# A routed feed-forward behind attention: two listed tiles of two halves for three whole ones, and the last tile's output scattered in two pieces

## The chip, the cores and the metric

The kernel runs on one core of one Trainium2 chip. The metric is the device time of one execution in microseconds; lower is better. The time to compare with is the median of three runs. The engines are named as in the profile: PE (TensorE matmuls), PEld (its weight loads), DVE (VectorE), ACT (ScalarE), POOL (GpSimd) and SP (SyncE, which here only issues DMAs).

## The reference

```python
def _attn_ref(q, k, v, g_q, g_k):            # q, k, v: (8, 12, 448, 64)
    q_n, k_n = (rmsnorm(q, g_q), rmsnorm(k, g_k))
    scores = 1.0 / np.sqrt(64) * np.matmul(q_n, k_n.transpose(0, 1, 3, 2))
    ...
    return np.matmul(softmax, v)

def _moe_ref(x, w_gate, w1_dense, w2_dense, w1, w2):   # x: 3584 tokens x 768
    y_dense = np.maximum(x @ w1_dense, 0.0) @ w2_dense  # hidden size 512
    logits = x @ w_gate                                 # 8 experts
    expert_idx = np.argmax(logits, axis=1)
    ...
    for e in range(E):
        mask = expert_idx == e
        h = np.maximum(x[mask] @ w1[e], 0.0)
        y_moe[mask] = gate_w[mask, None] * (h @ w2[e])
    return (y_dense + y_moe).astype(np.float32)
```

Attention of 96 heads gives 3584 tokens of 768 features. Every token goes through a dense feed-forward and through one of eight experts, which its logits choose; the sum of both is written to the output. The inputs are one fixed draw.

## The kernel before, in words

**Two stages.** In the first stage (up to about 230 us) the kernel computes attention, the logits, the choice of the expert and the hidden layer of the dense feed-forward, and writes each token as a record (its 768 features, its 512 dense hidden values, its gate weight and its token number) into a DRAM tensor `records`, sorted by expert: each expert has a region of its own there. In the second stage it reads the records back in tiles of 128, runs the expert on each tile, and scatters the rows of the tile to the output by token number.

**The tiles of the second stage.** Tiles 0 to 15 are the first two full tiles of each expert, 16 to 23 the third one of each. Tiles 24 to 27 are made of two halves: 64 records of one expert and 64 of its neighbour. What an expert has beyond 3 1/2 tiles (448 tokens) goes to *listed* tiles, which are found at run time: `final_list` (L550) counts the tokens of each expert and `listed` (L491) writes, for each listed tile, the number of the expert (`expt`) and the place of its records (`unit`). Before the change a listed tile is 128 records of one expert, `ND` = 3 of them are always run (tiles 28, 29 and 30), and more would be run in `surplus` under a branch at the end (L997), which is taken if more than `ND` are listed.

**What one tile does.** `fetch` (L774) reads the place of the tile on SP and issues its DMAs: for most tiles one load of the records, which `turn` (L795) transposes on PE; for the late tiles a small load (gate weight and token number, L782) and a transposing DMA (L783). `gemm1` (L816) makes the hidden layer: for tiles 3 to 27 with the expert's weights standing (L838), for listed tiles with the tokens standing and the weights moving (L829, six matmuls of 512 columns); their expert's number is read into a register on PE, and the weights are addressed through it. `htrans` (L843) transposes the hidden layer of a listed tile (PE L852, ACT L853). `gemm2` (L855) runs eight matmuls of 384 columns for the dense part (L862) and as many for the expert (L873; sixteen of 64 tokens each, in pairs, where a tile has two halves). DVE then writes the sum to `ysb` (L881 for listed tiles, L883 for the others), and POOL scatters it to `out` (L886).

**The order.** Every engine runs its instructions in the order in which the program issues them. In `tiles` (L900) the step for tile t issues the fetch of tile t+4 or t+5, `turn` of t+2, `gemm1` of t+1, `gemm2` of t and `htrans` of t+1. The steps before tile 3 are in the hand-written order `AT["tail"]`, where `li` issues the instructions of `final_list`, on DVE, in three portions. `pair()` hands out two pairs of PSUM banks in turn, so that who writes a pair waits until the one before the last that used it has been read.

## Time and profile before

| | us |
|---|---|
| median of 3 runs | 371.98 |
| lowest and highest run | 369.56, 372.89 |
| the profiled execution | 369.48 |
| its span, from the first to the last instruction | 367.7 |
| mean granted TensorE clock, share of full speed | 0.997 |

The profile belongs to one execution. Its span is 1.8 us shorter than its time. Times of single instructions below count from the start of the span.

### The profile page before, as it was taken

The page shows a single profiled execution, that of the slowest core. Times are in us where ns is not written, and L with a number is a line of the kernel's source. Part 1 is how long each engine was busy: PE and PEld are TensorE (multiplying, and loading weights), DVE is VectorE, ACT ScalarE, POOL GpSimd, SP SyncE. Part 2 cuts the span into 40 slices and gives each one's busy share as a digit, 9 for nine tenths or more (in the row PEclk, how much of TensorE's full clock was granted, in tenths as well). Part 3 has the DMA queues.
Part 4 walks back from the last instruction along what each step waited for, and adds up shares of the span by engine and source line. Part 5 has one row for each costly group of instructions (what it writes and reads, how often), then busy time and mean ns, then how long its engine had stood idle before and what let it go on. Part 6 is the DMA issues. An engine that isn't in the chain of part 4 may idle for free. (4 is left out here: it accounts for less than half of the span.)

```text
span 367.7 us, 11921 instructions
## 1 busy us (share of the span) xinstructions
PE 328.4 (89%) x4715; PEld 220.9 (60%) x4715; DVE 219.4 (60%) x793; ACT 230.6 (63%) x365; POOL 214.0 (58%) x300
## 2 busy tenths in 40 slices
PE   0367889999899998999999988999999999999992
PEld 0145566665575655656656654677777777777651
DVE  4778999888798888978866354523332432222221
ACT  2368988998889988989888333444443543334330
POOL 7357687868987689879689053437613512232222
PEclk9999999999999999999999999999999999999998
DMA  5969999999999879993269999888994966557410
GB/s 193 304 204 191 296 279 237 309 296 290 274 296 277 287 207 205 328 274 131 68 113 214 263 277 226 299 294 267 307 288 107 259 182 191 151 149 194 132 71 31
DMA packets 55438, 82.38 MB, mean 224 GB/s; under 512 B 18412, under 2 KB 43500, under 8 KB 55376
## 3 DMA queue, kind: packets, MB, share of 16 engines
q1 hardware_dynamic: 43184, 44.29, 42.2%
q0 software_dynamic: 12192, 37.27, 38.5%
q8 instruction: 39, 0.64, 0.7%
q14 instruction: 23, 0.19, 0.2%
HBM read 69.31 MB, written 26.97 MB: 262 GB/s over the span
## 5 line engine op out<-in xcount | busy, mean ns | idle before, releaser
L332 ACT ACTIVATE xflat<-PS 128x896 bf16<-128x896 f32 x168 | 146.0, 918 | 20.8 <-PE PS L330 18.9
L284 POOL TENSOR_TENSOR xn<-weall,r 128x448 bf16<-128x448 f32 x91 | 83.1, 939 | 9.0 <-issue 3.2
L886 POOL DMA_INDIRECT out_dram<-xflat,rall x31 | 30.6, 989 | 88.9 <-DVE xflat L883 46.0
L330 PE MATMUL PS<-qT,kT 64*128 64x448 bf16 x384 | 70.0, 366 | 10.7 <-ACT xflat L332 8.3
L349 PE MATMUL PS<-va,xflat 128*128 128x65 bf16 (+1 forms) x1536 | 75.9, 195 | 1.2 <-DVE rall L375 0.5
L349 PEld LDWEIGHTS <-xflat 128*128 128x128 bf16 (+1 forms) x1536 | 60.4, 97 | 23.1 <-issue 13.5
L263 DVE BATCH_NORM_STATS2 st<-weall 128x6 f32<-128x128 f32 x336 | 70.9, 279 | 4.0 <-DMA weall<-in_k_dram 3.7
L883 DVE SCALAR_TENSOR_TENSOR xflat<-PS,rall,xflat 128x768 f32<-128x768 f32 x25 | 25.4, 1018 | 77.2 <-ACT xflat L866 38.0
L479 POOL DMA_INDIRECT records<-rall,slot x32 | 32.6, 1018 | 23.9 <-ACT rall L612 13.1
L862 PE MATMUL PS<-wd,xflat 128*128 128x384 bf16 x248 | 45.5, 326 | 0.8 <-ACT heT L853 0.8
L873 PE MATMUL PS<-weall,heT 128*128 128x384 bf16 (+2 forms) x280 | 45.5, 327 | 0.2 <-ACT heT L853 0.2
L607 PE MATMUL PS<-wd,xT 128*128 128x512 bf16 x168 | 41.1, 380 | 1.2 <-ACT rall L612 1.2
L330 PEld LDWEIGHTS <-kT 64*128 64x128 bf16 x384 | 22.4, 95 | 27.7 <-issue 22.3
L838 PE MATMUL PS<-xflat,weall 128*128 128x128 bf16 (+1 forms) x696 | 38.7, 213 | 0.0
L375 DVE TENSOR_TENSOR rall<-PS,inv 128x256 bf16<-128x256 f32 x96 | 36.2, 419 | 2.0 <-DVE inv L381 0.4
L838 PEld LDWEIGHTS <-weall 128*128 128x128 bf16 x696 | 36.4, 115 | 1.5 <-issue 0.9
L873 PEld LDWEIGHTS <-heT 128*128 128x128 bf16 (+1 forms) x280 | 24.3, 100 | 16.7 <-issue 1.3
L842 ACT ACTIVATE heT<-PS 128x512 bf16<-128x512 f32 x25 | 14.9, 597 | 30.5 <-PE PS L838 28.9
L866 ACT COPY xflat<-PS 128x768 f32<-128x768 f32 x25 | 20.0, 799 | 18.9 <-PE PS L862 14.1
L295 PE MATMUL PS<-ident,xn 64*128 64x64 bf16 x672 | 17.8, 194 | 15.3 <-DVE xn L284 12.2
L862 PEld LDWEIGHTS <-xflat 128*128 128x128 bf16 x248 | 23.0, 98 | 13.9 <-issue 1.0
L803 ACT COPY xflat<-PS 128x512 bf16<-128x512 bf16 x22 | 12.9, 585 | 24.1 <-PE PS L802 24.0
(129 smaller groups left out, 347.2 us busy)
## 6 DMA issues: line engine op xcount, KB each, us to landing
weall<-in_q_dram SPq DMA_DIRECT2D x24, 448.0 KB, 8.9
weall<-in_k_dram SPq DMA_DIRECT2D x11, 896.0 KB, 10.2
rall<-records SPq DMA_DIRECT2D x18, 352.0 KB, 7.7
weall<-in_v_dram SPq DMA_DIRECT2D x48, 128.0 KB, 3.5
weall<-in_moe_w_dram POOLq DMA_DIRECT2D x8, 768.0 KB, 10.9
weall<-in_v_dram SPq DMA_DIRECT2D x48, 96.0 KB, 5.4
weall<-in_moe_w_dram POOLq DMA_DIRECT2D x12, 256.0 KB, 10.3
weall<-in_moe_w_dram POOLq DMA_DIRECT2D x8, 384.0 KB, 9.8
```

Of the source, the lines that this page charges most:

```text
L263: return [lambda s=s: nc.vector.bn_stats(sts[g][:, "qk".index(name), s].rearrange("p h c -> p (h c)"), xin[name, g].rearrange("p h (s d) - ...
L284: (eng or nc.gpsimd).tensor_tensor(xn[name, g][:, :, hh], xin[name, g][:, hh].rearrange("p (s d) -> p s d", d=D), r[:, "qk".index(name), : ...
L330: nc.tensor.matmul(ps[:, hh, :S], kT[row, c:c + P], qT[row, r], start=(n == 0), stop=(n == len(mm) - 1), skip_group_check=True)
L332: nc.scalar.activation(x, ps[:, :, :S], AF.Exp, scale=scale)
L349: nc.tensor.matmul(av[:, hh, m], exs[g, s][rows_, hh, QC[m]:QC[m] + P], va[rows_, s, hh, :De], start=(first and s == full[0] and m == m0), ...
L375: nc.vector.tensor_tensor(x[:, 2 * hh + r], av[:, hh, :, :D].rearrange("p m (a i) -> p m a i", a=2), inv[:, hh].unsqueeze(3).to_broadcast( ...
L479: i = nc.gpsimd.indirect_dma_start(out=rec, out_offset=bass.IndirectOffsetOnAxis(ap=slot[b % 2][:, m:m + 1], axis=0), in_=rb[b % 3][:, m], ...
L607: nc.tensor.matmul(W[:, bank], turnedx(b, kk, m), wd1[:, kk], start=(kk == 0), stop=(kk == KD - 1))
L838: nc.tensor.matmul(he[:, i * P + own.start:i * P + own.stop], weight(t, a, 0, kk * F + i, FT), xRs[t][:, kk, own], start=(i == 0 and a == ...
L862: nc.tensor.matmul(yps[t][:, dd, :HD], xRs[t][:, KD + i], wd2[:, i, dd * HD:(dd + 1) * HD], start=(i == 0), stop=(i == FT - 1 and not one_ ...
L873: nc.tensor.matmul(yp[own, dd, :HD], heTs[t][:, i, own], weight(t, a, 1, i * Dm + dd * HD), start=(i == 0 and not one_sum), stop=(i == FT ...
L886: i = nc.gpsimd.indirect_dma_start(out=out, out_offset=bass.IndirectOffsetOnAxis(ap=got(t)[:, GO + 1:GO + 2].bitcast(I32), axis=0), in_=ys ...
```

## The change

Listed tiles are now made of two halves of 64 records, each with an expert of its own, and two of them are run always (tiles 28 and 29). The list is written in halves, up to 50 of them instead of 27 tiles. The first half of a listed tile uses its expert's weights through a register on PE as before; the weights of the second half's expert are first copied by DVE to a fixed place (`hold`): those of the first layer into `wd1`, those of the second into a part of `xT` (tile 28) or of `rall` (tile 29). In `gemm1` and `gemm2` of listed tiles each matmul of 128 tokens becomes two of 64. The last tile has a `gemm2` of its own, `last_gemm2`: it does the 384 output features of one half after those of the other, and copies and scatters each alone; POOL makes the two row numbers for that.

```diff
--- before.py
+++ after.py
@@ -120,9 +120,9 @@
     EL = 4
     NE, NS = 2 * E, 3 * E
     NM = NS + E // 2
-    ND = 3
+    ND = 2
     LAST = NM + ND
-    NF = N // P - 1
+    NF = 25
     NT = NM + NF
     BLANK = 2 * E * RT
     MAGIC = 12582912.0
@@ -509,7 +508,6 @@
             lambda: ge.tensor_reduce(o[1], t[1], AX.X, ALU.add),
             lambda: ge.tensor_tensor(o[2], o[1], iot[:, :n], ALU.add),
             lambda: ge.tensor_scalar(o[2], o[2], first[:, :1], None, op0=ALU.add),
-            lambda: ge.tensor_scalar(o[2], o[2], 2.0, 1.0, op0=ALU.mult, op1=ALU.add),
             lambda: ge.tensor_scalar(unit[:, row, :n], o[2], float(BLANK), None, op0=ALU.min)]
 
     def counted(b, c):
@@ -564,12 +562,12 @@
             lambda: ve.tensor_scalar(back, took, 2.0, -float(BLANK), op0=ALU.mult, op1=ALU.add)
         ] + halves(unit[:, 1, :E]) + [
             lambda: ve.tensor_tensor(first, took, one_, ALU.add),
-            lambda: ve.tensor_scalar(last, n, -0.5, 1.0 / P, op0=ALU.add, op1=ALU.mult),
-            lambda: ve.tensor_scalar(last, last, MAGIC, MAGIC, op0=ALU.add, op1=ALU.subtract),
-            lambda: ve.tensor_tensor(last, last, first, ALU.max),
             lambda: ve.tensor_tensor(one_, first, up, ALU.is_lt),
             lambda: ve.tensor_scalar(back, first, 2.0, -float(BLANK), op0=ALU.mult, op1=ALU.add)
-        ] + halves(unit[:, 1, E:2 * E]) + listed(NF, RT, first, last, 2, pre) + [
+        ] + halves(unit[:, 1, E:2 * E]) + rounded(last, n, D, True) + [
+            lambda: ve.tensor_scalar(first, first, 2.0, 1.0, op0=ALU.mult, op1=ALU.add),
+            lambda: ve.tensor_tensor(last, last, first, ALU.max)
+        ] + listed(2 * NF, 2 * RT, first, last, 2, pre) + [
             lambda: ve.tensor_copy(total, pre[:, E - 1:])]
 
     def gaps(ix):
@@ -739,14 +737,15 @@
     SETTLE = (TT + 6, TT + 12, TT + 16, TT + 20, TT + 24, LAST - 2)
     hsur = const.tile([P, FT, P], BF16)
     gix = const.tile([P, E], I32)
+    idx2 = const.tile([P, 2], I32)
 
 
     def parts(t):
-        return [slice(0, D), slice(D, P)] if NS <= order[t] < NM else [slice(0, P)]
+        return [slice(0, D), slice(D, P)] if order[t] >= NS else [slice(0, P)]
 
     def place(t, a):
         return ((0, t) if t < NE else (1, t - NE) if t < NS else (1, E + 2 * (t - NS) + a)
-                if t < NM else (2, t - NM))
+                if t < NM else (2, 2 * (t - NM) + a))
 
     def expert(t, a=0):
 
@@ -769,7 +768,7 @@
 
     def by_dma(t):
 
-        return t >= NS - 3 and len(parts(t)) == 1
+        return t >= NS - 3 and not NS <= order[t] < NM
 
     def fetch(t):
         xRs[t] = xrb[t % 5]
@@ -780,7 +779,7 @@
             r = r.rearrange("o p c -> (o p) c")
             if by_dma(t):
                 ins = [nc.sync.dma_start(got(t)[own, GO:GO + 2], r[:, GO:GO + 2]),
-                       nc.sync.dma_start_transpose(xRs[t], r[:, :GO].bitcast(BF16))]
+                       nc.sync.dma_start_transpose(xRs[t][:, :, own], r[:, :GO].bitcast(BF16))]
             else:
                 ins = [nc.sync.dma_start(got(t)[own], r)]
             e = expert(order[t], a)
@@ -802,12 +801,30 @@
                 nc.tensor.transpose(o[:, k], x[:, a * KD + k], ident)
             copy(xRs[t][:, a * KD:a * KD + n], o)
 
+    def other(t):
+
+
+        w2 = (xT.rearrange("p k n s -> p (k n s)")[:, :FT * Dm].rearrange("p (i d) -> p i d", i=FT)
+              if t % 2 == 0 else rall[:, 7:11, :GO].bitcast(BF16)[:, :, :Dm])
+        return wd1, w2
+
+    def hold(t):
+
+        n = 2 * (t - NM) + 1
+        e = nc.vector.value_load(expt[:, 2, n:n + 1], min_val=0, max_val=E - 1)
+        for n, w in enumerate(other(t)):
+            nc.vector.tensor_copy(w, we[:, bass.ds(e, 1), n].rearrange(
+                "p o (i f) -> p (o i) f", i=w.shape[1]))
+
     def weight(t, a, n, c, step=1):
 
         w = step * (P - 1) + 1 if step > 1 else F if n == 0 else HD
         e = expert(order[t], a)
         if e is not None:
             return we[:, e, n, c:c + w:step]
+        if a:
+            i, c = divmod(c, F if n == 0 else Dm)
+            return other(t)[n][:, i, c:c + w]
         return we[:, bass.ds(eregs[t], 1), n, c:c + w].rearrange("p o f -> p (o f)")
 
     def token_major(t):
@@ -815,8 +832,8 @@
 
     def gemm1(t, heT=None):
         if t >= NM:
-            eregs[t] = nc.tensor.value_load(expt[:, 2, t - NM:t - NM + 1], min_val=0,
-                                            max_val=E - 1)
+            n = 2 * (t - NM)
+            eregs[t] = nc.tensor.value_load(expt[:, 2, n:n + 1], min_val=0, max_val=E - 1)
         heTs[t] = sb.tile([P, FT, P], BF16, tag="qT", name="heT") if heT is None else heT
         if t < TT:
             mids[t] = pair()
@@ -826,8 +843,9 @@
             claim("01"[t % 2], ("he", t))
         if token_major(t):
             for kk in range(KD):
-                nc.tensor.matmul(he, xRs[t][:, kk], weight(t, 0, 0, kk * F),
-                                 start=(kk == 0), stop=(kk == KD - 1))
+                for a, own in enumerate(parts(t)):
+                    nc.tensor.matmul(he[own], xRs[t][:, kk, own], weight(t, a, 0, kk * F),
+                                     start=(kk == 0), stop=(kk == KD - 1))
             hes[t] = sb.tile([P, F], BF16, tag="xv", name="hs")
             nc.scalar.activation(hes[t], he, AF.Relu, scale=gate(t))
         else:
@@ -852,7 +870,32 @@
             nc.tensor.transpose(hp[:, i], hs[:, i], ident)
         nc.scalar.copy(heTs[t], hp)
 
+    def last_gemm2(t):
+
+        ys, yp = ysb[t % 3], pair()
+        for dd in range(2):
+            nc.gpsimd.tensor_scalar(idx2[:, dd:dd + 1], got(t)[:, GO + 1:GO + 2].bitcast(I32),
+                                    2.0, float(dd), op0=ALU.mult, op1=ALU.add)
+        for dd in range(2):
+            for i in range(FT):
+                nc.tensor.matmul(yp[:, dd, :HD], xRs[t][:, KD + i],
+                                 wd2[:, i, dd * HD:(dd + 1) * HD], start=(i == 0), stop=False)
+            for i in range(FT):
+                for a, own in enumerate(parts(t)):
+                    nc.tensor.matmul(yp[own, dd, :HD], heTs[t][:, i, own],
+                                     weight(t, a, 1, i * Dm + dd * HD), start=False,
+                                     stop=(i == FT - 1), skip_group_check=False)
+            nc.vector.tensor_copy(ys[:, dd], yp[:, dd, :HD])
+            i = nc.gpsimd.indirect_dma_start(
+                out=out.rearrange("n (a d) -> (n a) d", a=2),
+                out_offset=bass.IndirectOffsetOnAxis(ap=idx2[:, dd:dd + 1], axis=0),
+                in_=ys[:, dd], in_offset=None, bounds_check=2 * N - 1, oob_is_err=False)
+            apart(i, stores, "each token has one slot")
+            stores.append(i)
+
     def gemm2(t, part=None):
+        if t == LAST - 1:
+            return last_gemm2(t)
 
         one_sum = token_major(t)
         if part != 1:
@@ -911,6 +954,8 @@
                 turn(t + 2)
             if t + 1 < LAST:
                 gemm1(t + 1)
+            if NM <= t + 2 < LAST:
+                hold(t + 2)
             gemm2(t)
             if t + 1 < LAST:
                 htrans(t + 1)
@@ -920,6 +965,7 @@
         for t in range(LAST, NT):
             fetch(t)
             turn(t)
+            hold(t)
             gemm1(t, hsur)
             htrans(t)
             gemm2(t)
@@ -993,8 +1039,8 @@
         attention()
         tail_and_slots()
 
-    ntot = nc.values_load(total, min_val=0, max_val=NF)
-    with tc.If(ntot > ND):
+    ntot = nc.values_load(total, min_val=0, max_val=2 * NF)
+    with tc.If(ntot > 2 * ND):
         with tc.manual_schedule(engines=ENGINES):
             surplus()
```

In the order of the engines, three places show it. First PE, at the start of the first layer of tile 28. Before, six matmuls move the weights of one expert past 128 tokens (`xflat` holds the tokens, `weall` the experts' weights; ISA computes an address from the register):

```order
L818 TENSOR_LOAD expt
L818 ISA x2
L829 LDWEIGHTS xflat
L829 ISA
L829 MATMUL PS<-weall,xflat 128x512
```

Now each has become two of 64 tokens, the second with the weights that DVE has copied into `wd1` (here `wd_81`):

```order
L836 TENSOR_LOAD expt
L836 ISA x2
L847 LDWEIGHTS xflat
L847 ISA
L847 MATMUL PS<-weall,xflat 64x512
L847 LDWEIGHTS xflat
L847 MATMUL PS<-wd_81,xflat 64x512
```

The number of columns that move is the same for each matmul; the number of matmuls has doubled. Second DVE, at the end of its program. Before, the sums of tiles 25, 26 and 27 (L883) stand one behind the other, and then the copies of the three listed tiles:

```order
L803 COPY xflat<-PS 128x768
L883 SCALAR_TENSOR_TENSOR xflat<-PS,rall,xflat 128x768 x3
L881 COPY xflat<-PS 128x768 x3
L996 TENSOR_LOAD total
L997 COMPARE_AND_BRANCH
```

Now a register load and two copies of 3072 elements each stand between the sums of tiles 25 and 26 (`hold` of tile 28):

```order
L926 SCALAR_TENSOR_TENSOR xflat<-PS,rall,xflat 128x768
L814 TENSOR_LOAD expt
L814 ISA x2
L816 ISA
L816 COPY wd_81<-weall 128x3072
L816 ISA
L816 COPY xT<-weall 128x3072
L926 SCALAR_TENSOR_TENSOR xflat<-PS,rall,xflat 128x768
```

The same rows stand again between the sums of tiles 26 and 27 (`hold` of tile 29, with `rall` in place of `xT`), and behind them are one copy of 768 columns (L924, tile 28) and two of 384 (L888, tile 29) where three of 768 were. Third POOL, at the end of its program, before:

```order
L886 DMA out_dram<-xflat,rall 3584x768
L896 DMA weall<-in_moe_w_dram 128x1536
L886 DMA out_dram<-xflat,rall 3584x768 x17
L996 TENSOR_LOAD total
L997 COMPARE_AND_BRANCH
```

and now:

```order
L939 DMA weall<-in_moe_w_dram 128x1536
L929 DMA out_dram<-xflat,rall 3584x768 x15
L877 TENSOR_SCALAR idx_104<-rall 128x1 x2
L889 DMA out_dram<-xflat,idx_104 7168x384 x2
L1042 TENSOR_LOAD total
L1043 COMPARE_AND_BRANCH
```

Two whole scatters are gone, and two small operations and two scatters of half rows stand at the end.

## Rows read from the trace of the kernel before

**Rows 1.** Windows, tiles 3 to 27: length, busy us of PE, PEld, DVE, ACT, POOL; clock

```profile
237.00:345.00 108.00, 108.00 (x1281) 82.09 (x1279) 33.09 (x44) 44.01 (x67) 37.50 (x42) 1.00 0.76 216
```

**Rows 2.** Timeline of the last tiles: start, duration, what, [idle before <-releaser]

```profile
340.90 1.02 DVE L883 SCALAR_TENSOR_TENSOR xflat<-PS,rall,xflat 128x768 f32<-128x768 f32 x1 [3.02 <-ACT xflat L866]
...
344.84 1.46 PE L829 MATMUL PS<-weall,xflat 128*128 x6
345.10 1.02 DVE L883 SCALAR_TENSOR_TENSOR xflat<-PS,rall,xflat 128x768 f32<-128x768 f32 x1 [3.18 <-PE PS L873]
...
346.39 0.98 POOL L886 DMA_INDIRECT out_dram<-xflat,rall  x1 [3.22 <-DVE xflat L883]
...
349.49 1.46 PE L829 MATMUL PS<-weall,xflat 128*128 x6
...
353.61 1.46 PE L829 MATMUL PS<-weall,xflat 128*128 x6
...
357.73 1.46 PE L862 MATMUL PS<-wd,xflat 128*128 128x384 bf16 x8
357.98 0.58 ACT L853 COPY heT<-PS 128x512 bf16<-128x512 bf16 x1 [2.14 <-PE PS L852]
...
359.03 1.46 PE L873 MATMUL PS<-weall,heT 128*128 x8
360.53 0.96 DVE L881 COPY xflat<-PS 128x768 f32<-128x768 f32 x1 [1.86 <-PE PS L873]
361.76 0.98 POOL L886 DMA_INDIRECT out_dram<-xflat,rall  x1 [1.85 <-DVEq L997]
```

**Rows 3.** DMA issues: count, KB, median us from issue to landing

```profile
out_dram<-xflat,rall POOLq DMA_INDIRECT x31, 3.8
...
xflat<-records SPq DMA_TRANSPOSE x9, 3.5
```

**Rows 4.** Timeline around one tile of two halves: PE, and PEld

```profile
308.91 1.46 PE L862 MATMUL PS<-wd,xflat 128*128 128x384 bf16 x8
310.31 1.49 PE L873 MATMUL PS<-weall,heT 128*64 128x384 bf16 x16
311.73 1.79 PE L838 MATMUL PS<-xflat,weall 128*128 128x64 bf16 x48
...
310.30 1.12 PEld L873 LDWEIGHTS <-heT 128*64 128x64 bf16 x16 [0.32 <-issue]
```

**Rows 5.** Lines by form: out<-in count | busy us, mean ns | idle before

```profile
L803 DVE COPY xflat<-PS 128x768 bf16<-128x768 bf16 x22 | 12.1, 549 | 9.3 <-PE PS L802 9.3
L881 DVE COPY xflat<-PS 128x768 f32<-128x768 f32 x6 | 5.7, 958 | 11.4 <-PE PS L873 11.3
L316 DVE COPY kT<-PS 128x128 bf16<-128x128 bf16 x24 | 5.1, 213 | 0.0
...
L504 DVE TENSOR_TENSOR t<-iot,f 1x216 f32<-1x216 f32 x1 | 0.4, 361 | 0.0
```

**Rows 6.** Timeline of PE, DVE and POOL where DVE makes the list

```profile
235.40 0.98 POOL L479 DMA_INDIRECT records<-rall,slot  x1 [1.85 <-ACT rall L612]
...
235.98 0.40 DVE L512 TENSOR_SCALAR o<-o 1x27 f32<-1x27 f32 x1
...
237.69 1.50 PE L838 MATMUL PS<-xflat,weall 128*128 128x128 bf16 x24
237.89 0.96 DVE L881 COPY xflat<-PS 128x768 f32<-128x768 f32 x1
...
239.03 0.72 PE L802 MATMUL PS<-ident,rall 128*128 128x128 bf16 x10
```

**Rows 7.** Timeline of SP's queue: the transposing loads of tiles 28 and 29

```profile
331.10 1.39 SPq L783 DMA_TRANSPOSE xflat<-records  x1
...
335.04 1.37 SPq L783 DMA_TRANSPOSE xflat<-records  x1
```

**Rows 8.** POOL's small operations: times of L447 on one line of the timeline

```profile
221.91 0.22 POOL L447 TENSOR_SCALAR rall<-dbase 128x4 int32<-128x4 f32 x1
```

## Prediction

> **What bounds the kernel now.** I read the windows first: from 237 to 345 us PE is busy in all 108 us, at full clock, while the other engines have room [rows 1]. So in the second stage each microsecond that PE is given or spared comes out at the end. Then I read the timeline of the last tiles [rows 2]. What the reader is to see: PE runs on without a wait from the first listed tile (344.84) to its last block (359.03, which with its 1.46 us ends at 360.49); then come one after the other the DVE copy of the last result (360.53 to 361.49), the issue of its scatter on POOL (361.76 to 362.74), and the landing. The end is thus PE's end plus a chain of about 5 us to the last landing, which is in part the scatter's 3.8 us [rows 3]. The chain of waits says nothing of use here, since it holds only the last scatter.
>
> **Whether the work fits.** By the reference's own choice of experts, counted from its fixed draw in float32, the experts get 409, 528, 432, 430, 448, 366, 478 and 493 tokens. Beyond 448 that is three tiles of 128 (one each for 528, 478, 493), and in halves of 64 it is 2 + 1 + 1 = 4, just what two tiles hold. The trace agrees for the tiles: 31 scatters [rows 3] are 28 tiles and three listed ones, so the branch to `surplus` was not taken, and the expert with 448 did not get a 449th token on the chip. A fifth half would need 19 more tokens for the expert with 493, or 34 for the one with 478, or 49 for the one with 528.
>
> **The sum, step by step, against the profiled execution (369.48 us).**
>
> 1. One listed tile goes: a `gemm1`, a `gemm2` and an `htrans`. From the start of `gemm1` of tile 30 (353.61) to the start of the dense block of the same tile (357.73) lie exactly one `gemm2`, one `htrans` and that `gemm1` [rows 2]: -4.12 us. What DVE, ACT and POOL did for it lay beside PE's work and brings nothing of its own.
>
> 2. The remaining matmuls become pairs of 64 tokens. The row for a half tile shows what that costs: 16 matmuls of 64 take 1.42 us from their start to the start of the next block (310.31 to 311.73), where eight of 128 take 1.30 (357.73 to 359.03), so the two of a pair run side by side; but the dense block ahead of them takes 1.40 instead of 1.30 (308.91 to 310.31), and the weight loads stand 0.32 us idle at the change [rows 2, 4]. So a block of halves costs 0.10 + 0.12 = 0.22 us, whatever is in it. There are five new ones: `gemm1` of tiles 28 and 29, the expert block of tile 28, and the two expert blocks of tile 29, which `last_gemm2` takes apart: 5 x 0.22 = +1.1 us. From both sides: 0, if neighbouring blocks share the change, and +5.2 if nothing runs side by side (third rival). `gemm1` blocks of halves occur nowhere in the trace; six matmuls of 512 columns move the same 3072 as eight of 384, so I take the same price.
>
> 3. In `last_gemm2` only four dense matmuls (0.65 us, half of 1.30) stand between `htrans` and the first expert block, which needs ACT's copy. That copy ended at 358.56, 0.83 us after the dense block began (357.73) [rows 2]; with 0.04 us for the signal (as between PE's end at 360.49 and DVE's start at 360.53) PE waits 0.22 us: +0.22.
>
> 4. At the end the copy is of 384 columns. The copy of 768 takes 958 ns; what does not grow with its size is about 0.15 us, from 549 ns for 768 and 213 ns for 128 bf16 columns [rows 5]. So half takes 0.15 + 0.40 = 0.55: -0.4. The first half's scatter (0.98 us on POOL) starts some 1.3 us before the second's, and the two row numbers (0.22 us each [rows 8]) are made before, behind tile 28's scatter; neither should hold the second up, but the margin is a few tenths. For the smaller landing I take nothing; it can be -0.5 us, or +0.3 if the two scatters get in each other's way.
>
> 5. The list. DVE builds it just before it must copy the result of tile 2 (237.89 to 238.85), and PE's transposes at 239.03 wait for that copy, as they overwrite its banks; PE comes there straight from its block at 237.69, so the margin is 0.1 to 0.2 us [rows 6]. Four of the list's instructions grow from 216 to 400 elements. At 361 ns for 216 [rows 5], less the fixed 0.15, one element takes about 1 ns: 4 x 0.19 = +0.76; four others grow by 23 elements (+0.1), one small one moves into this portion (+0.1), and L512 with its 0.40 us goes. List and copy are some 0.5 us late, and PE waits 0.4: +0.4. Its bounds are 0 and +0.9.
>    L512 takes 0.40 us for 27 elements and ends at 236.38, in the moment in which the scatter on POOL ends (235.40 + 0.98) [rows 6]. The Trainium skill ("SBUF — State Buffer", section "Who interferes with whom") says that DVE in a two-port mode and POOL shut each other out for a whole instruction. By that rule the wait would fall to the next instruction of that kind instead of going with L512, PE would wait 0.8 us, and the sum would be 0.4 us less gain; the trace agrees for this one row.
>
> 6. `hold`: two copies of 3072 bf16 elements per listed tile on DVE. No row shows a copy from SBUF to SBUF. Between bf16 rows of 768 and 128 one element takes 0.525 ns, so 3072 take 1.75 us; by the f32 row (1.06 ns) 3.39 [rows 5]; the lower end is 0. I take 1.75, the same operation on the same type. For tile 28 DVE is idle from 341.92 to 345.10: the first copy is there at 343.7, before 344.84, and the sum of tile 26 starts 0.3 us late, which nobody waits for. Queued behind it are the sum of tile 26 and its scatter. For tile 29 the first copy may only start when `gemm1` of 28 has read `wd1`, about 346.4, and perhaps, with POOL's scatter in its way, at 347.37; it ends at 348.2 to 349.1, and `gemm1` of 29 is due at 349.7 [rows 2]. Hidden, with 0.6 to 1.5 us to spare; behind the second copy waits the sum of tile 27, needed only by the last tile's blocks after 354. Cost 0.
>    The Trainium skill ("VectorE: DVE Perf Modes", section "The perf-mode tier table") gives copies of bf16 within SBUF four elements a cycle; an estimate from that page (3072 / 4 at 0.96 GHz, and 0.15 fixed) is 0.95 us each. No run here shows it; by it the sum stays as it is.
>
> 7. SP: each listed tile now has two small loads and two transposing loads. The first transposing load of tile 28 is issued at 331.10, of 29 at 335.04, 1.4 us each [rows 7]; with the second pair, and 3.5 us to land [rows 3], tile 28 is there by about 340 and 29 by 344, needed at 344.84 and 349.7. Cost 0.
>
> Sum: -4.12 + 1.1 + 0.22 - 0.4 + 0.4 = -2.8 us, or 366.7 us for an execution like the profiled one. The median before, 371.98, lies 2.5 us above that execution, so on the median I forecast 371.98 - 2.8 = 369.2.
>
> **The rivals.**
>
> - *The change of shape costs little.* If blocks of halves next to each other share it and the list stays under its cover (both terms 0), the gain is 4.12 - 0.22 + 0.4 = 4.3 us: 367.7. For it: the two last blocks of tile 29 are only 0.65 us long and may begin behind a wait anyway. Against it: 0.32 us of idle weight loads at the change [rows 4].
> - *DVE becomes the bound.* At 3.39 us a copy, `hold` of 28 lasts from 341.92 to 348.7; the sum of 26 ends at 349.7, the first copy for 29 at 353.1, and PE waits there, 3.4 us in all: 369.2 + 3.4 = 372.6. It decides above about 2.5 us a copy. Against it: bf16 copies from PSUM already run twice as fast as that [rows 5].
> - *Slower: pairs do not run side by side.* The two matmuls of a pair now move different tensors, one of them addressed through a register with an instruction in between. If they ran one after the other, four blocks of 1.30 us would take twice that, +5.2: 369.2 + 5.2 = 374.4, slower than before by 2.4. It decides as soon as a pair takes over 1.5 times a single one. Against it: the half tile, whose pairs also move two experts' weights [rows 4].
> - *The change does not do what it says.* A fifth half sends the program into `surplus`, 23 tiles of at least 4.12 us: some 95 us more. The counts above speak against it.
>
> **How the numbers follow.** The forecast has 0.53, the cheap change of shape 0.25, DVE 0.10, the pairs 0.09, `surplus` 0.03. About 1% (3.7 us) is what a measurement of this kernel can tell from no change; its three runs spread over 3.3. Faster by over 1% means below 368.3: two thirds of the first rival (0.17) and a quarter of the forecast's own spread of about 1.5 us (0.14), 0.31 in all. Slower by over 1% means above 375.7: `surplus`, a quarter of the pairs' case, and a little of DVE's: 0.07. The rest, 0.62, is within. The range runs from 366.5, the first rival with a faster landing, to 372.8, which takes in DVE's case; it leaves the last two rivals out.
>
> **What would show it.** Right: the weight loads stand about 0.3 us idle at each block of halves of tiles 28 and 29; from `gemm1` of 28 to PE's end 12.9 us instead of 15.65; the DVE copies of 3072 under 2 us and no wait of PE for them; PE idle about 0.4 us before the transposes that stood at 239.03; 29 whole scatters and two of half rows. Wrong: a PE wait for DVE at `gemm1` of tile 29 over 0.5 us, blocks of halves over 2 us, or a second scatter held up on POOL by over 0.5 us.

## The result, and the profile after

The kernel after takes 368.55 us (median of 10 runs, 367.29 to 369.59), the kernel before beside it 371.77 (10 runs, 369.56 to 373.86). The ratio is 0.9917, with a 95% interval of 0.9887 to 0.9946: 3.2 us less, within 1% of no change, as forecast (369.2). The profiled execution of after took 368.61 us, with a span of 366.9. Some executions of a program run in a slower state; the medians and ratios of the experiments leave these out.

The timeline of the last tiles comes first, as it did before. It answers to [rows 2, 4]; matmuls of 64 tokens stand in it one by one where their operands alternate.

```profile
343.91 0.96 DVE L816 COPY wd<-weall 128x3072 bf16 x1
344.11 1.75 POOL L929 DMA_INDIRECT out_dram<-xflat,rall  x1 [3.52 <-DVE xflat L926]
...
345.45 1.46 PE L916 MATMUL PS<-weall,heT 128*128 128x384 bf16 x8
...
346.85 1.00 PEld L847 LDWEIGHTS <-xflat 128*64 128x64 bf16 x12 [0.32 <-issue]
346.85 0.40 PE L847 MATMUL PS<-weall,xflat 128*64 x1
...
348.27 1.47 PE L905 MATMUL PS<-wd,xflat 128*128 128x384 bf16 x8
348.31 1.15 POOL L929 DMA_INDIRECT out_dram<-xflat,rall  x1 [2.44 <-DVE xflat L926]
348.38 0.96 DVE L816 COPY wd<-weall 128x3072 bf16 x1 [0.35 <-PE PS L847]
...
351.09 0.42 PE L870 MATMUL PS<-ident,hs 128*128 128x128 bf16 x4
...
352.97 1.47 PE L905 MATMUL PS<-wd,xflat 128*128 128x384 bf16 x8
...
354.37 0.35 PE L916 MATMUL PS<-weall,heT 128*64 x1
...
355.79 0.42 PE L870 MATMUL PS<-ident,hs 128*128 128x128 bf16 x4
...
356.05 0.81 PE L881 MATMUL PS<-wd,xflat 128*128 128x384 bf16 x4
356.30 0.58 ACT L871 COPY heT<-PS 128x512 bf16<-128x512 bf16 x1 [2.54 <-PE PS L870]
...
357.04 0.35 PE L885 MATMUL PS<-rall,heT 128*64 128x384 bf16 x1
...
357.92 0.56 DVE L888 COPY xflat<-PS 128x384 f32<-128x384 f32 x1 [1.06 <-PE PS L885]
...
359.08 0.33 PE L885 MATMUL PS<-rall,heT 128*64 128x384 bf16 x1
359.28 1.03 POOL L889 DMA_INDIRECT out_dram<-xflat,idx  x1 [0.66 <-POOL idx L877]
359.45 0.56 DVE L888 COPY xflat<-PS 128x384 f32<-128x384 f32 x1 [0.97 <-PE PS L885]
360.78 0.98 POOL L889 DMA_INDIRECT out_dram<-xflat,idx  x1 [0.47 <-issue]
```

Tile 28 begins at 346.85 and PE ends at 359.08 + 0.33 = 359.41, 12.56 us later. Before it was 15.65: 344.84 to 360.49 [rows 2]. The last scatter starts 1.37 us behind PE's end (1.27 before). The listed tiles' copies on DVE take 0.96 us each, and PE waits for none of them. Where a copy and a scatter meet, POOL's instruction grows to 1.75 or 1.15 us from 0.98.

The second view is the windows of the stretch of [rows 1], with the same columns.

```profile
237.00:345.00 108.00, 107.05 (x1276) 81.42 (x1274) 35.14 (x54) 43.44 (x66) 37.85 (x44) 1.00 0.75 210
```

PE now misses 0.95 us here, and its timeline shows where: `gemm2` of tile 15 waits for ACT, which overwrites a buffer that a scatter must have read first (ACT's copy starts 3.17 us behind the start of that scatter, and 3.18 behind it in before). POOL issued this scatter at 283.81 only, since it had stood at a `drain` (L922), an instruction that the kernel issues in front of six of the scatters and that took 14.48 us here.

```profile
283.81 0.99 POOL L929 DMA_INDIRECT out_dram<-xflat,rall  x1 [13.79 <-issue]
...
287.83 1.46 PE L905 MATMUL PS<-wd,xflat 128*128 128x384 bf16 x8 [0.90 <-ACT xflat L909]
```

The change doesn't touch this place, and the size goes with the length of that drain from one profile to the next: no wait where it took up to 13.7 us (12.93 in before, 12.76 in `e3_idx_early`, 13.62 in `e6_hold3`), 0.59 us at 14.16 (`e8_list_behind`), 0.80 at 14.38 (`e4_short_list`), 0.90 here, 1.27 at 14.85 (`e7_shared_copy`). What makes the drain longer or shorter is open. The first stage ended 0.64 us later as well. So the two profiled spans differ by 0.8 us only (367.7 and 366.9), where the medians differ by 3.2: single executions are compared below by the stretch that an edit touches, not by their spans.

The third view is the timeline where DVE makes the list, answering to [rows 6].

```profile
238.33 1.50 PE L856 MATMUL PS<-xflat,weall 128*128 128x128 bf16 x24
239.89 0.72 PE L801 MATMUL PS<-ident,rall 128*128 128x128 bf16 x10
...
238.89 0.95 DVE L924 COPY xflat<-PS 128x768 f32<-128x768 f32 x1
```

From the block of tile 3 to the transposes of tile 5 lie 1.56 us, where it was 1.34 (237.69 to 239.03 [rows 6]): PE waits 0.22 us for DVE's copy, which ends at 239.84. The lines by form give the price of a 400-element operation of the list, beside the 361 ns for 216 in [rows 5]:

```profile
L503 DVE TENSOR_TENSOR t<-iot,f 1x400 f32<-1x400 f32 x1 | 0.6, 561 | 0.0
```

### The profile page after: what moved, and what is told of

Its sections match the earlier page's. It is cut to its first block, busy times and chain, and to the rows that moved or that the text cites. A ratio compares the mean times of both kernels' runs of the same rounds, so it can differ in the third digit from the quotient of the medians.

```text
span 366.9 us, 11931 instructions
## 1 busy us (share of the span) xinstructions
PE 326.2 (89%) x4717; PEld 219.2 (60%) x4717; DVE 222.8 (61%) x797; ACT 229.2 (62%) x363; POOL 215.6 (59%) x302
## 4 chain that ended last, share of the span: by engine, by line
PE 50%; DVE 5%; POOL 3%; ACT 2%; issue 1%; POOLq 0%; ACTq 0%
PE PS L916 10%; PE PS L905 10%; PE PS L856 9%; PE PS L349 5%; PE PS L605 4%; PE PS L801 3%; PE PS L330 2%; POOL xn L284 2%; PE PS L847 2%; PE PS L391 1%; DVE rall L375 1%; POOL records L479 1%; DVE st L263 1%; ACT rall L610 1%; PE PS L412 1%
## 5 line engine op out<-in xcount | busy, mean ns | idle before, releaser
L929 POOL DMA_INDIRECT out_dram<-xflat,rall x29 | 29.6, 1022 | 84.3 <-DVE xflat L926 55.7
L905 PE MATMUL PS<-wd,xflat 128*128 128x384 bf16 x232 | 42.6, 326 | 1.7 <-ACT xflat L909 0.9
L916 PE MATMUL PS<-weall,heT 128*128 128x384 bf16 (+2 forms) x264 | 42.6, 327 | 0.2 <-ACT heT L871 0.2
L916 PEld LDWEIGHTS <-heT 128*128 128x128 bf16 (+1 forms) x272 | 22.8, 101 | 15.7 <-issue 1.6
L905 PEld LDWEIGHTS <-xflat 128*128 128x128 bf16 x232 | 21.3, 98 | 14.3 <-issue 2.8
L295 PEld LDWEIGHTS <-xn 64*128 64x128 bf16 x672 | 16.3, 98 | 19.9 <-POOL xn L284 14.2
```

The source lines that it names most:

```text
L295: nc.tensor.transpose(Wb[:, r, c:c + D], xn[name, g][half, s].rearrange("p h d -> p (h d)"), ident[half, half])
L905: nc.tensor.matmul(yps[t][:, dd, :HD], xRs[t][:, KD + i], wd2[:, i, dd * HD:(dd + 1) * HD], start=(i == 0), stop=(i == FT - 1 and not one_ ...
L916: nc.tensor.matmul(yp[own, dd, :HD], heTs[t][:, i, own], weight(t, a, 1, i * Dm + dd * HD), start=(i == 0 and not one_sum), stop=(i == FT ...
```

## The experiments

Twelve kernels ran, in three groups, each on one chip; the kernel before, run beside them, had medians of 380.72, 371.32 and 381.02 us. In the expectations the letters stand for theories: A is the prediction's own accounting by terms, the others are the rivals that they name. The stretch "from tile 28" begins with the first matmul of `gemm1` of tile 28. Unless another is named, an edit is made in the kernel after.

**The removed tile alone** (`e5_two_whole`, an edit of the kernel before: two whole listed tiles are run, the third one's tokens are left out).

```diff
-    ND = 3
+    ND = 2
-    NF = N // P - 1
+    NF = N // P - 2
-    with tc.If(ntot > ND):
+    with tc.If(ntot > ND + 1):
```

> The kernel before with two whole listed tiles instead of three (the third one's tokens, some 45 of the expert with 493, stay unwritten; the branch limit is raised so that nothing else runs). Theory A (the gain is one listed tile, less about 0.2 us for each new block of halves, and the split of the last output brings next to nothing): from the first matmul of tile 28 to PE's end 11.5 us, against 15.65 before and 12.56 after; the last scatter starts 1.27 us behind PE's end; the time 4.1 us under before, ratio 0.989. Theory B (blocks of halves cost nothing and what is missing to 4.1 us went into the earlier stages): PE's stretch is as after, 12.5 us.

Measured: ratio 0.9866 [0.98, 0.9932]. The timeline shows the stretch and its end:

```profile
357.30 1.46 PE L829 MATMUL PS<-weall,xflat 128*128 x6
...
361.41 0.41 PE L852 MATMUL PS<-ident,hs 128*128 128x128 bf16 x4
361.95 1.46 PE L829 MATMUL PS<-weall,xflat 128*128 x6
363.25 1.46 PE L862 MATMUL PS<-wd,xflat 128*128 128x384 bf16 x8
...
367.37 1.46 PE L873 MATMUL PS<-weall,heT 128*128 x8
...
370.10 0.98 POOL L886 DMA_INDIRECT out_dram<-xflat,rall  x1 [1.79 <-DVE xflat L881]
```

From tile 28 (357.30) to PE's end (367.37 + 1.46 = 368.83) it is 11.53 us, 4.12 less than before, and the last scatter again starts 1.27 behind it. Term 1 is exact, and nothing hid it.

**Halves or whole matmuls, split or not** (`e1_whole`: listed tiles use whole matmuls, so the second half of each gets the first one's expert; `e2_nosplit`: the last tile's output is made and scattered whole).

```diff
# e1_whole, in three loops of gemm1, last_gemm2 and gemm2
+    def sides(t):
+        return parts(t) if order[t] < NM else [slice(0, P)]
-                for a, own in enumerate(parts(t)):
+                for a, own in enumerate(sides(t)):
# e2_nosplit
-        if t == LAST - 1:
-            return last_gemm2(t)
```

> The changed kernel with its listed tiles computed by matmuls of 128 tokens with the first half's expert, loads and DVE copies as they are (the second half's tokens get the wrong expert's output). Theory A: the new blocks of halves and their changes of shape go, PE's stretch from tile 28 to its end is 11.9 us instead of 12.56, and the idle 0.3 us of the weight loads at each block is gone. Theory B: 12.5 us.

> The changed kernel with the ordinary second layer, one copy and one scatter for the last tile. Theory A: PE's stretch 12.1 us, the last scatter starts 1.27 us behind PE's end, that is 13.4 us behind tile 28's first matmul, 0.6 us sooner than after (13.93). Theory C (the split pays, since copy and scatter of one half lie beside the matmuls of the other): the last scatter starts 14.4 us behind tile 28's first matmul, and the span ends later.

| from tile 28, us | to PE's end | to the last scatter | to the end of the span |
|---|---|---|---|
| before | 15.65 | 16.92 | 22.86 |
| `e5_two_whole` | 11.53 | 12.80 | 17.90 |
| `e1_whole`: split, no halves | 11.99 | 13.57 | 17.96 |
| `e2_nosplit`: halves, no split | 12.10 | 13.38 | 19.53 |
| after: both | 12.56 | 13.93 | 20.05 |

The spans are 367.7, 375.2, 371.3, 371.9 and 366.9 us. The lines for `e1_whole`, then `e2_nosplit`:

```profile
353.34 1.46 PE L850 MATMUL PS<-weall,xflat 128*128 x6
...
357.45 0.41 PE L873 MATMUL PS<-ident,hs 128*128 128x128 bf16 x4
358.12 1.46 PE L850 MATMUL PS<-weall,xflat 128*128 x6 [0.25 <-issue]
...
364.52 0.81 PE L888 MATMUL PS<-weall,heT 128*128 x4
```

```profile
352.37 0.40 PE L847 MATMUL PS<-weall,xflat 128*64 x1
...
364.14 0.33 PE L914 MATMUL PS<-rall,heT 128*64 128x384 bf16 x1
```

Without the split the halves cost 12.10 - 11.53 = 0.57 us in this stretch. The split adds 12.56 - 12.10 = 0.46: 0.34 is PE's wait for `heT` in front of the first expert block of tile 29 (0.99 us behind its dense block where the work is 0.65, in `e1_whole` as in after), and 0.12 the second block of halves, into which the split takes the last tile apart. `e1_whole` has no halves there, and yet lies 0.46 above `e5_two_whole` as well. That is a coincidence: besides the same 0.34 it has 0.13 at another place, where PE stands idle 0.25 us for nothing that the profile shows, so that from the transposes to `gemm1` of tile 29 it takes 0.67 us (357.45 to 358.12) instead of 0.54 (361.41 to 361.95 in `e5_two_whole`). Another 0.10 of the halves lies just ahead of the stretch, in the block before tile 28 (1.40 us instead of 1.30, from 345.45 to 346.85). The split gives nothing back: the last scatter starts 0.55 us later with it than without (13.93 and 13.38).

**Why the scatter of the split starts late.** The half copy ends at 360.01, and its scatter starts at 360.78, 0.77 behind it; before, it was 0.27 (361.49 to 361.76 [rows 2]). Three edits tried this.

`e3_idx_early` makes the two row numbers on POOL ahead of tile 28's scatter instead of behind it; `e7_shared_copy` gives up the split and lets ACT and DVE copy a half each.

```diff
# e3_idx_early: these lines move from last_gemm2 into the gemm2 of tile 28, with got(t + 1)
-        for dd in range(2):
-            nc.gpsimd.tensor_scalar(idx2[:, dd:dd + 1], got(t)[:, GO + 1:GO + 2].bitcast(I32),
-                                    2.0, float(dd), op0=ALU.mult, op1=ALU.add)
# e7_shared_copy, with the edit of e2_nosplit
-        if one_sum:
+        if t == LAST - 1:
+            nc.scalar.copy(ys[:, 0], yp[:, 0, :HD])
+            nc.vector.tensor_copy(ys[:, 1], yp[:, 1, :HD])
+        elif one_sum:
```

> The changed kernel with POOL's two row number operations ahead of tile 28's scatter instead of behind it. Theory A (the split's gain is lost because POOL is late with the first of the two scatters): the first half's scatter starts 0.3 us behind its copy, the second one's 0.9 us behind PE's end instead of 1.37, 13.4 us behind tile 28's first matmul. Theory C': the two scatters hold each other up in any case, and the second still starts 1.3 us behind PE's end.

> The changed kernel without the split of the last tile, its result copied half by ACT and half by DVE at once, and scattered whole. Theory A: PE's stretch 12.1 us, the scatter starts 0.9 us behind PE's end, 13.0 us behind tile 28's first matmul, against 13.93 after. Theory C (scattering in halves pays): no earlier end of the span than after, counted from that matmul (20.05 us).

Both missed. In `e3_idx_early` (378.34 us, one run) the last scatter starts 1.37 behind PE's end, as in after; in `e7_shared_copy` (369.71, one run) 1.38, with 13.48 from tile 28, 0.78 behind the later of its two copies. It was therefore not the place of the row numbers. What led on is the list of everything on the line of these scatters, POOL's queue with it (count, durations least/median/most in ns, first and last start), of after:

```profile
L889 POOLq EVENT_SEMAPHORE  x2: 921/1158/1396, 357.1 to 359.1; - x2
```

Here a separate instruction holds the wait: 1396 ns from 357.1 to the end of the first copy, 921 ns from 359.1 to the end of the second, at 360.0. The scatter starts some 0.75 us behind that. The scatter of a half waits for DVE's copy, for DMAs and for POOL's own row numbers; that of `e7_shared_copy` for ACT, DVE and DMAs. A whole scatter waits for DVE and DMAs only. `e9_idx_dve` takes away POOL's part and leaves the rest:

```diff
-            nc.gpsimd.tensor_scalar(idx2[:, dd:dd + 1], got(t)[:, GO + 1:GO + 2].bitcast(I32),
+            nc.vector.tensor_scalar(idx2[:, dd:dd + 1], got(t)[:, GO + 1:GO + 2].bitcast(I32),
```

> The kernel after, with the two row numbers of the last tile's halves made on DVE instead of POOL, so that the two last scatters wait for DVE and for DMAs, and no longer for POOL's own operations besides. If the third semaphore is what puts the waits into an instruction of their own and so starts the scatter 0.77 us behind its copy: here each of the two starts about 0.28 us behind the end of its copy, the last one 0.9 us behind PE's end (1.37 in the kernel after) and 13.4 us behind the first matmul of tile 28 (13.93). The rival, that a scatter of half rows starts late whatever it waits for (or that POOL has to finish the first one's issue): 0.75 us or more behind the copy, 13.9 us. The time should be 0.5 us under the kernel after by the first, within what one run can't tell.

The same list of `e9_idx_dve`, and its timeline:

```profile
L889 POOLq EVENT_SEMAPHORE  x2: 17/17/17, 368.6 to 370.2; - x2
...
369.52 0.56 DVE L888 COPY xflat<-PS 128x384 f32<-128x384 f32 x1 [0.94 <-PE PS L885]
370.36 0.98 POOL L889 DMA_INDIRECT out_dram<-xflat,idx  x1 [0.64 <-DVE xflat L888]
371.05 0.56 DVE L888 COPY xflat<-PS 128x384 f32<-128x384 f32 x1 [0.97 <-PE PS L885]
371.89 0.98 POOL L889 DMA_INDIRECT out_dram<-xflat,idx  x1 [0.55 <-DVE xflat L888]
```

The long waits are gone from the separate instruction (17 ns each), and the scatters start 0.28 us behind their copies (370.08 to 370.36, 371.61 to 371.89). The last one starts 0.88 behind PE's end and 13.44 from tile 28, as the theory asked. So a scatter that waits for one producer more starts 0.5 us later; that it is the count of semaphores, rather than which engine it is, rests on this pair and `e7_shared_copy`. Its one run took 379.92 us beside a median of 381.02 for before, and from tile 28 to the end of the span it is 19.75: the 0.5 us doesn't come out. `e12_small_surplus` below says why.

**The list.** `e4_short_list` makes it 27 entries long (by the prediction's counts this input has four).

```diff
-        ] + listed(2 * NF, 2 * RT, first, last, 2, pre) + [
+        ] + listed(27, 2 * RT, first, last, 2, pre) + [
```

> The changed kernel with a list of 27 entries instead of 50 (only four are used). Theory A (the longer list on DVE delays the copy that PE's transposes of tile 5 wait for): from tile 3's first expert matmul to these transposes 1.34 us as before, instead of 1.56. Theory B (this wait has another cause): 1.5 us or more.

It has 1.34 us from tile 3 to tile 5 again, and took 368.36 us (one run). But the long list doesn't always show: of the other kernels that have it at this place, `e6_hold3` and `e7_shared_copy` had 1.57 and 1.56 us, and the six in the other two groups 1.34. In these six PE itself comes later: at the dense block of tile 2, ahead of the list's end, it waits 1.00 to 1.09 us for ACT's `heT` instead of 0.78 (after, `e6_hold3`, `e7_shared_copy`). So DVE's copy starts 0.25 to 0.33 us behind the block of tile 3, where it is 0.56 in after (238.33 to 238.89) and 0.20 in before (237.69 to 237.89 [rows 6]), and still ends in time. The wait in `e3_idx_early`:

```profile
245.17 1.30 PE L902 MATMUL PS<-wd,xflat 128*128 128x384 bf16 x7 [1.03 <-ACT heT L871]
```

The list thus makes the copy some 0.36 us late, and PE pays for it only where it comes early enough to notice.

`e8_list_behind` is `e7_shared_copy` with the list moved behind the copy that PE waits for:

```diff
-        ('se', 7, 2), ('tu', 7), ('li', 99), ('tt', 4), ('g2', 2, 1)],
+        ('se', 7, 2), ('tu', 7), ('tt', 4), ('g2', 2, 1), ('li', 99)],
```

> As the run with the shared copy, and DVE makes the list behind the copy of tile 2's result instead of ahead of it. Theory A: both waits are gone, the transposes of tile 5 follow 1.34 us behind tile 3's first expert matmul, the stretch at the end is 13.0 us; 1.1 to 1.2 us under the changed kernel, ratio to before about 0.988. Theory B: the stages ahead of tile 28 decide, and the ratio stays at 0.992.

It was worse, which neither theory held: ratio 1.0012 [0.9986, 1.0038]. The transposes come without a wait (at 240.22, 1.34 us behind the block), and the next block pays more:

```profile
243.66 1.50 PE L856 MATMUL PS<-xflat,weall 128*128 128x128 bf16 x24 [2.71 <-DVE g L583]
```

The operation of L583 reads a PSUM bank that this block overwrites, and it stands behind the list on DVE. The edit traded 0.22 us for 2.71.

**The copies of `hold`, three times over** (`e6_hold3`).

```diff
-            nc.vector.tensor_copy(w, we[:, bass.ds(e, 1), n].rearrange(
-                "p o (i f) -> p (o i) f", i=w.shape[1]))
+            for _ in range(3):
+                nc.vector.tensor_copy(w, we[:, bass.ds(e, 1), n].rearrange(
+                    "p o (i f) -> p (o i) f", i=w.shape[1]))
```

> The changed kernel with each of the four weight copies on DVE done three times. Theory A (the copies are hidden with a margin of about 2 us at tile 29): the copies of tile 28 still end in time, PE waits about 1.4 us for those of tile 29, and PE's stretch from tile 28 to its end is 14.0 us instead of 12.56. Rival (PE never comes near a wait for DVE here): 12.6 us.

```profile
342.82 2.95 DVE L817 COPY wd<-weall 128x3072 bf16 x3
343.02 1.88 POOL L930 DMA_INDIRECT out_dram<-xflat,rall  x1 [3.52 <-DVE xflat L927]
...
349.47 2.94 DVE L817 COPY wd<-weall 128x3072 bf16 x3
...
352.46 0.38 PE L848 MATMUL PS<-wd,xflat 128*64 128x512 bf16 x1 [1.68 <-DVE wd L817]
```

At 2.95 us per weight PE waits 1.68 us at `gemm1` of tile 29, exactly where the prediction's second rival put it, and the stretch to PE's end grows from 12.56 to 14.55; the last scatter starts 3.36 us behind that, since DVE's sum of tile 27 is late too, and with it the scatters that stand ahead on POOL (those of tiles 27 and 28 start at 356.47 and 360.69). 371.0 us (one run). The rival was a real mechanism; its price of 3.39 us a copy was not.

**The end of the program, and a shorter version.** In after the span ends 20.05 - 13.93 = 6.12 us behind the start of the last scatter; before it was 5.94, in `e5_two_whole` 5.10. The list of line L1025 (before) and L1071 (after), the last of the program, shows who is last there. The first of the two DRAINs of PE's queue, and the first of SP's three, come when that queue has done all else; SP's stands behind its waits for the landings. Before, then after:

```profile
L1025 SPq DRAIN  x3: 7/7/12, 366.8 to 367.1; - x3
...
L1025 PEldq DRAIN  x2: 8/8/8, 364.1 to 367.2; - x2
```

```profile
L1071 SPq DRAIN  x3: 7/7/13, 364.8 to 366.3; - x3
...
L1071 PEldq DRAIN  x2: 8/8/8, 366.1 to 366.4; - x2
```

Before, PE was done at 364.1 and SP at 366.8: the landing sets the end. After, SP is done at 364.8, and PE only at 366.1. PE's branch over the code of `surplus`, on the line of the `If`, accounts for a part of it (after, then `e12_small_surplus`, which cuts that code from 23 tiles to one; this input does not run it):

```profile
L1043 PEldq COMPARE_BRANCH  x1: 3940/3940/3940, 358.6 to 358.6; - x1
```

```diff
-        for t in range(LAST, NT):
+        for t in range(LAST, LAST + 1):
```

> The kernel after with the code behind the branch cut to one tile (instead of 23), which this input does not run: the same work, and less code to jump over. If PE's way over that code sets the program's end (in the kernel after PE's last instruction comes 3.3 us behind the end of its branch, and later than the waits of SP's queue for the landings): PE's branch takes well under 3.9 us or its last instruction follows within 1.5 us, the end comes 5.0 us behind the start of the last scatter instead of 6.1, and the median is 1 us under the kernel after beside it. If the length of the skipped code plays no part: branch and gap stay at 3.9 and 3.3 us, 6.1 us from scatter to end, and the same median.

```profile
L1043 PEldq COMPARE_BRANCH  x1: 251/251/251, 366.2 to 366.2; - x1
...
L1071 SPq DRAIN  x3: 7/7/13, 373.6 to 373.9; - x3
...
L1071 PEldq DRAIN  x2: 13/692/1372, 367.8 to 374.0; - x2
```

And a line from the timeline of PE's last blocks in `e12_small_surplus`:

```profile
366.94 0.32 PE L885 MATMUL PS<-weall,heT 128*64 x1 [0.95 <-PEq L1043]
```

The branch takes 0.25 us instead of 3.9, PE's first DRAIN starts at 367.8, and SP is last again (373.6). From the start of the last scatter to the end it is 3.98 us, still less than the 5.0 expected. But the branch now begins 3.0 us before PE's end (366.2 and 369.15) instead of 0.8 (358.6 and 359.41), and the profile puts a wait of 0.95 us in PE's last blocks down to it. From tile 28 to PE's end it is 13.75 us, so that of 2.1 us won behind the scatter 1.2 are spent ahead of it. The ratio is 0.9915 [0.9878, 0.9952].

The other two runs on that chip are after again and the version without either small loss, `e10_whole_short` (the edits of `e2_nosplit` and `e4_short_list` together).

> The kernel after with the last tile stored whole (no split into halves of 384 features) and the list cut to 27 entries (entries beyond the 27th half tile, which this input does not have, can't be listed). If the changes of shape and the third semaphore cost what the earlier runs showed, PE's stretch from tile 28's first matmul to its end is 12.1 us, the last scatter starts 13.4 us behind that matmul (13.93 in the kernel after), and from the block of tile 3 to that of tile 5 lie 1.34 us (1.56): together 0.75 us under the kernel after, a ratio to the kernel before near 0.990. The rival, that these stretches trade against waits elsewhere (the drain of tile 15, the end of the program): the stretches are as said, but the median lies within 0.3 us of the kernel after.

> The kernel after, unchanged, beside the others on one chip: a ratio to the kernel before of 0.990 to 0.994. If the 1.06 us between 284.6 and 288 in its first profile belongs to that execution and not to the kernel, another profile shows another size there, while the stretch from tile 28's first matmul to PE's end is 12.55 us again and the second stage's other pieces are as before. If it belongs to the kernel, it is there again with 0.9 us or more.

`e10_whole_short` has 12.09 us from tile 28 to PE's end, 13.37 to the last scatter, and 1.34 at the list, all as expected; the ratio is 0.9935 [0.9892, 0.9979]. `e11_after_again` has 0.9899 [0.9836, 0.9963]. These three ratios, taken on one chip, can't be told apart: no version was shown to beat after. The 0.56 us by which `e10_whole_short` starts its last scatter earlier does not show at the end: from tile 28 to the end of the span, the kernels in which, as in after, PE's DRAIN comes last have 19.36 (`e7_shared_copy`) to 20.05 us (after), with no order by when their last scatter starts: 19.44 with 13.37 to the scatter (`e10_whole_short`), 19.75 with 13.44 (`e9_idx_dve`), 19.46 with 13.94 (`e4_short_list`). The wait at tile 15, which the expectations put at 1.06 us in all, is not in the profile of `e11_after_again`, as its first theory asked, nor in that of `e3_idx_early`; the drains took 12.78 and 12.76 us there.

## Why the prediction came out right

Its sum was -2.8 us. In the profiles, from tile 28 to the end of the span it is 22.86 - 20.05 = 2.81 less; 0.10 just ahead of tile 28 and 0.22 at the list go off that, which leaves -2.5, beside a difference of the medians of -3.2 (by the interval -4.2 to -2.0). The total is thus right, and its parts less so. How near it came is in part luck: `e4_short_list`, whose last tiles do the same work as those of after, has 19.46 us from tile 28 to the end of the span, where after has 20.05.

1. *One tile goes*, -4.12: measured alone, 15.65 - 11.53 = 4.12. Right.
2. *Five blocks of halves*, +1.1: the mechanism was right, the size was not: 0.57 + 0.10 without the split and 0.12 more with it, 0.79. `gemm1` of tile 28 and the expert block of tile 28 pay the full 0.22 each: 0.10 in the block ahead (345.45 to 346.85, 352.97 to 354.37: 1.40 each) and 0.12 in their own (1.42), with weight loads 0.32 us idle at the first, as in [rows 4]. But `gemm1` of tile 29 follows the transposes and pays 0.04: transposes and block take 1.88 us (351.09 to 352.97), where two whole ones take 1.84 (361.41 to 363.25 in `e5_two_whole`). The rest, some 0.3, lies in the last tile, for the most part in its first expert block and its second dense block, which take 0.77 and 0.76 us to the next block instead of 0.65 (from 357.04 to 357.81, and on to 358.57). The first rival, with this term at 0, was right for `gemm1` of tile 29 alone.
3. *The wait for `heT`*, +0.22: it cost 0.34. From the dense block of tile 29 to its first expert block lie 0.99 us (356.05 to 357.04), where its own work is 0.65; ACT's copy ends at 356.88, and the first matmul starts 0.16 behind it. The mechanism was right, the signal was taken too short (0.04).
4. *The last copy is half*, -0.4: this is the step that failed. The copy took 0.56, as worked out (0.55). But "neither should hold the second up" did not hold: the scatter waits for POOL's row numbers besides, and starts 0.77 behind the copy instead of 0.27. The term is +0.10. The margin of "a few tenths" named the risk without its mechanism; it was a cost of the wait itself, not of the queue, as `e9_idx_dve` shows. The 0.5 us is just the size that the prediction named as a sign of being wrong. One premise failed with it: that the program ends with the last landing. In after SP, which waits for the landings, is done at 364.8, and PE's last instruction comes at 366.1, so that neither the gain hoped for at the last scatter nor the loss found there shows in the end.
5. *The list*, +0.4: 0.22 in after, `e6_hold3` and `e7_shared_copy`, nothing in the others. An operation of 400 elements takes 561 ns, as reckoned (361 for 216, and 0.19 us for the rest); what was off is the delay of the copy, 0.36 us instead of some 0.5, of which 0.14 was covered. The further 0.4 us by the Trainium skill ("SBUF — State Buffer", section "Who interferes with whom") did not come at PE; the scatter beside the list took 1.27 us (236.04), where that of before took 0.98. Elsewhere the trace agrees with that rule: DVE's bf16 copies stretch the scatters beside them from 0.98 to 1.75 and 1.15 us.
6. *The copies of `hold`*, hidden: right, with 0.96 us each instead of the 1.75 taken. The estimate of 0.95 from the Trainium skill ("VectorE: DVE Perf Modes", section "The perf-mode tier table") was the right one, four elements a cycle; taking the price from PSUM copies for a copy within SBUF was the poorer choice, though the cover made it harmless.
7. *SP*: the four transposing loads of the listed tiles are issued from 333.01 to 341.50, and PE waits for none. Right.

The errors nearly cancel, and that they do is luck: terms 2 and 3 cost 1.13 together instead of 1.32, the list 0.2 less than forecast, the fourth term 0.5 more, and 0.18 more lies between the last scatter's start and the end. The other rivals did not come: the pairs run side by side, PE did not wait for DVE's weight copies, and `surplus` was not entered: the DMA issues are 29 whole scatters and two of halves, beside the 31 of [rows 3]. One count of the prediction is off by one, and nothing rests on it: a fifth half would need 20 more tokens for the expert with 493, or 35 for the one with 478, since a half more holds them up to 512.

## What to carry to other kernels

Price a removed block by the stretch between two blocks on the engine that is never idle: that number came out to the hundredth, while everything at the seams (a change of shape, a wait for one producer more, a wait on another engine's copy) was off by a quarter to a half, and one term in its sign. When a store at the end of the chain is made smaller, look at what it waits for before counting the bytes: half the copy saved 0.40 us, and one more producer to wait for cost 0.50. And look at which engine's queue ends last, by its last instructions: once the stores are no longer the last, work on them brings nothing that these runs could show.

## What the runs showed of the hardware that was not expected

- An indirect store on POOL that waits for one producer more than usual (its own engine's operations, or ACT beside DVE) gets its wait in a separate instruction, and starts about 0.77 us behind the last producer instead of 0.28.
- PE's branch over unexecuted code takes time with the code's length: 3.94 us over 23 tiles, 0.25 over one. Behind it PE has two short waits. Its last instruction, the DRAIN, followed these at once in before, `e5_two_whole` and `e1_whole`, but some 3.3 us later in after (362.8 to 366.1), and 2.8 to 3.5 us later in the nine others that keep the 23 tiles. In the first three the listed tiles, and the tiles in the code that is jumped over, are of whole matmuls, in the others of halves. Whether the length of that code on PE decides this second part, or the halves ahead of the branch, is open; with one tile and halves (`e12_small_surplus`) it is 1.1 us.
- A bf16 copy of 3072 elements a partition within SBUF takes DVE 0.96 us, and scatters that POOL issues meanwhile take up to 1.88 us (`e6_hold3`) instead of 0.98.
